# The end of a fused attention and soft-MoE kernel put in another order: last group's maxima, combine transposes, splits, and layer two

## The chip, the core and the metric

The kernel runs on one core of a Trainium2 chip. The metric is the device time of one execution in microseconds. Three runs of the kernel before the change took 1510.94, 1512.75 and 1512.81 us; the median is 1512.75 us. One further execution was recorded by the hardware profiler.

## The reference

The outputs of an attention without softmax, times its gate `u`, are the tokens of a soft mixture of experts. 8 batches of 2496 positions give N = 19968 tokens of 256 numbers; there are 8 experts with 4 slots each, so 32 slots, and hidden layers of 1024.

```python
scores = (1.0 / S) * np.matmul(z, z.transpose(0, 2, 1))
attn = np.maximum(scores, 0.0) ** 2
x = (u * np.matmul(attn, v)).reshape(N, D)

logits = x @ phi                       # N x 32
d = exp(logits - logits.max(0));  d /= d.sum(0) + 1e-09   # over tokens
slot_input = (d.T @ x).reshape(E, S_per_e, D)
for e in range(E):
    h = np.maximum(slot_input[e] @ w1[e], 0.0)
    slot_out[e] = h @ w2[e]
c = exp(logits - logits.max(1));  c /= c.sum(1) + 1e-09   # over slots
return c @ slot_out
```

The maxima and sums of `d` run over all tokens. So the experts can start only when the last token's logits are known, and every output needs the experts.

## The kernel before

**Attention.** Each batch is cut into chunks of up to 512 queries; the last batch ends in two chunks of 256. A chunk is worked off in 5 key steps `p` of two half steps `s`. In a half step PE multiplies scores (`sc`), ACT and DVE square and split them in a high and a low part (`ph`, `pl`), and PE adds their products with `v` into `acc` in PSUM. At a chunk's end `finish_chunk` multiplies `acc` with `ut` on DVE into `xg`, the tokens.

**The soft-MoE work beside it.** Tokens are gathered in groups of 1024 (`xg_[q]`, q from 0 to 18, and a last group of 512). For each full group the generator `groups(q)` makes logits, running maxima (`runmax`), exponentials, transposes of the tokens (`tr` into `xt`, line 313 on), the combine weights (kept unnormalised by slot but divided by their sum, in `cw`), and running slot sums, which `add_up` (line 385) rescales and adds into `slot_acc`. The generator stops at each `yield`; its steps are called from the list `work`, one per half step with `2 * p + s > 1`. All these use one two-bank PSUM buffer of the pool `ms_ps`, in turn.

**The order.** `InOrder` (line 47) wraps PE, ACT and DVE. Every operation called through it keeps the order in which the program names it on its engine. Almost all operations go through it, so the profile shows them at line 47 and they are told apart by their tiles. `between_last(s)` (line 510) puts work of its own between the last two half steps.

**The last group** (from line 552): logits `lg_last`, maximum, exponential `E_last`, transposes of both, slot sums `sl_last` added to the rescaled `slot_acc`, then a normalisation by the sums (`pn`) and by the maxima of the four row groups (`fac`, `fpad`, `fsel`). It ends in `sT` (a part of the tile `tiny`), the slots' inputs in the layout that layer 1 needs.

**The experts.** `layer1(eg, h)` makes 16 matmuls of 512 columns in four blocks (`h`), with a `relu` on ACT; `turn_hidden` transposes a block (`hT`) with a copy on DVE; `layer2(c, eg)` makes 64 small matmuls into `po`, for half `c` of the 256 output columns.

**Outputs.** `outputs(c, ·)` spreads `po` over the partitions (`so`) and splits it into `soh` and `sol`. `turn(k, ·)` transposes 8 of the 39 blocks of `cw` (`cT`), which `split_hi` (ACT) and `split_lo` (DVE) split into `ch` and `cl`. `tokens(c, u, ·)` is one unit: 12 matmuls into `pf`, a copy of one half by ACT and of the other by DVE into `ot`, and an output transfer by SP. `UNITS` has two units of 0.5 MiB, eight of 1 MiB, and one of 0.75 MiB; they are run for both halves `c`, 22 transfers in all. `ot` has four buffers. Before the change, turns and splits of `cw` stand between the units, and `layer2(1, ·)` between units 0 and 4:

```python
    outputs(0, ms_ps.tile([P, 512], F32, tag="ms", name="so4_0"))
    tokens(0, UNITS[0], some)
    tokens(0, UNITS[1], some)
    layer2(1, 0)
    next_turn(1)
    tokens(0, UNITS[2], some)
    layer2(1, 1)
    tokens(0, UNITS[3], some)
    next_turn(2)
```

**Weights.** 32 loads of 0.5 MiB (`w`): 16 in the last chunks into buffers of the pool `blk`, and behind them ten into the pool `wx` and six more into `blk` as attention's tiles come free; `ch` and `cl` take buffers of `blk` too.

Of the kernel before, what the change touches and what calls it, by code (L numbers as in the profile page):

```python
# [50 lines left out]
def attn_soft_moe_kernel(ctx, tc, uT, v, zz, phi, ww, outT):  # L51
# [63 lines left out]
    esel = cpool.tile([P, E_, NS], F32, name="esel")  # L115
# [9 lines left out]
    def constants():  # L125
# [3 lines left out]
        nc.gpsimd.memset(esel, 0.0)  # L129
        nc.gpsimd.memset(rsel, 0.0)  # L130
        for h in range(4):
            rows = slice(h * NS, (h + 1) * NS)
            nc.gpsimd.tensor_copy(
                esel[rows, :, 0:SE], ident[rows, rows].rearrange("k (e s) -> k e s", s=SE)
            )
            nc.gpsimd.tensor_copy(ssel[rows], ident[rows, rows])
# [126 lines left out]
    def finish_chunk(b, ch, acc):  # L263
# [3 lines left out]
        while s < n:  # L267
# [4 lines left out]
            dve.tensor_mul(xg_[q][:, :, o : o + w], acc[:, :, s : s + w], ut[:, :, s : s + w])  # L272
# [22 lines left out]
    def groups(q):  # L295
# [38 lines left out]
        yield  # L334

# [74 lines left out]
    def turn(k, ps):  # L410

        for i in range(min(8, NG - 8 * k)):
            for h, rows in enumerate(HALF):
                pe.transpose(
                    ps[:, h, i * 64 : (i + 1) * 64], cw[rows, 8 * k + i], ident[rows, rows]
                )
        return ps
# [3 lines left out]
    def split_hi(k, ps):  # L421
        hi = blk.tile([P, 8, P], F32R, tag="blk", name=f"ch_{k}")
        ng = min(8, NG - 8 * k)
        px = ps[:, :, : ng * 64].rearrange("p h (g n) -> p h g n", g=ng)
        act.copy(hi[:, :ng].rearrange("p g (h n) -> p h g n", h=2), px)
        parts[k] = hi, px

    def split_lo(k):
        hi, px = parts[k]
        lo = blk.tile([P, 8, P], F32R, tag="blk", name=f"cl_{k}")  # L430
        ng = min(8, NG - 8 * k)
        dve.tensor_sub(
            lo[:, :ng].rearrange("p g (h n) -> p h g n", h=2), px,
            f32(hi[:, :ng]).rearrange("p g (h n) -> p h g n", h=2),
        )
# [72 lines left out]
    xps, turned = [], []  # L508
# [44 lines left out]
    x = xg_.pop(q)  # L553
    lg = sc_ps.tile([P, QC], F32, tag="sc", name="lg_last")
    for c in range(2):
# [5 lines left out]
    turn_x(xps[0], x, 0, range(2, 4))  # L561

    tiny = wk.tile([P, 2, 1024], F32, tag="xg", name="tiny").rearrange("p a b -> p (a b)")
    sT = tiny[:, 0:512].rearrange("p (c k) -> p c k", c=2)
    fpad = tiny[:, 512:768]
    fsel = tiny[:, 768:800]
    fac, rs = tiny[:, 800:801], tiny[:, 802:804]
    mrow = tiny[0:1, 1024 : 1024 + 5 * NS].rearrange("p (t s) -> p t s", s=NS)
    ET = tiny[:, 1280:1408]
    nc.gpsimd.memset(sT, 0.0)  # L570
    m = wk.tile([P, 5], F32, tag="m", name="m_last")
    L = wk.tile([P, 2 * P], F32, tag="L", name="L_last", bufs=1)[:, 0:P]
    E = wk.tile([P, 2 * P], F32, tag="E", name="E_last", bufs=1)[:, 0:P]
    mnew, mold = runmax[q % 2], runmax[(q + 1) % 2]
    snew, sold = slot_acc[q % 2], slot_acc[(q + 1) % 2]
    dve.reduce_max(m[:, 0:1], lg[:, 0:P], axis=AX.X)
    dve.tensor_max(mnew, m[:, 0:1], mold)
    dve.tensor_scalar_mul(m[:, 1:2], mnew, -1.0)
    dve.tensor_sub(m[:, 2:3], mold, mnew)
    act.activation(E, lg[:, 0:P], AF.Exp, bias=m[:, 1:2], accum_out=m[:, 4:5])  # L580
    act.activation(m[:, 3:4], m[:, 2:3], AF.Exp)
    dve.tensor_copy(L, lg[:, 0:P])


    pm = ms_ps.tile([P, 2, 512], F32, tag="ms", name="pm")
    pe.transpose(pm[0:1, 0, 0:P], mnew, ident)
    dve.tensor_reduce(
        mrow[:, 4], pm[0:1, 0, 0:P].rearrange("p (t s) -> p s t", s=NS), axis=AX.X, op=ALU.max
    )
    dve.tensor_copy(mrow[:, 0:4], mrow[:, 4].unsqueeze(1).to_broadcast([1, 4, NS]))  # L590
    et = sc_ps.tile([P, QC], F32, tag="sc", name="et_last")
    pe.transpose(et[:, 0:P], E, ident)
    dve.tensor_copy(ET, et[:, 0:P])
    pe.matmul(
        pm[:, 1, 0:1], mrow[:, 0:4].rearrange("p t s -> p (t s)"), one, start=True, stop=True
    )
    dve.tensor_sub(fac, mnew, pm[:, 1, 0:1])
    act.activation(fac, fac, AF.Exp)
    act.activation(fpad, esel.rearrange("k e q -> k (e q)"), AF.Copy, scale=fac)
    dve.tensor_scalar_mul(fsel, ssel, fac)  # L600
    sl = acc_ps.tile([P, 2, QC], F32, tag="acc", name="sl_last")
    for t in range(4):
        pe.matmul(
            sl[t * NS : (t + 1) * NS, 0, 0:D], ET[:, t * NS : (t + 1) * NS], xt[:, 0, t],
            start=True, stop=True,
        )
    dve.scalar_tensor_tensor(
        snew[:, D : D + 1], sold[:, D : D + 1], m[:, 3:4], m[:, 4:5], op0=ALU.mult, op1=ALU.add
    )
    dve.scalar_tensor_tensor(  # L610
        snew[:, 0:D], sold[:, 0:D], m[:, 3:4], sl[:, 0, 0:D], op0=ALU.mult, op1=ALU.add
    )

    pn = ms_ps.tile([P, 2, 512], F32, tag="ms", name="pn")
    for eg in range(2):
        pe.matmul(
# [215 lines left out]
```

## Time and profile before

| what | us |
|---|---|
| median of three runs | 1512.75 |
| the profiled execution's own time | 1512.82 |
| its span, first to last instruction | 1510.6 |
| PE busy | 1476.4 |
| DVE busy | 1107.5 |
| ACT busy | 1022.5 |
| last `acc` ended, `xg` started | 1421.27 |
| first matmul of layer 1 | 1428.15 |
| first output transfer issued | 1448.27 |
| bytes written | 20.45 MB |

The profile of an execution is a page of totals, and views of the same trace. The chain is the row of work that ended last, followed back from the end. The timeline lists instructions with the idle time before them and what released them in brackets. The windows give busy times of the engines in a stretch, with the clock that TensorE was granted (1.00 is full). PE is TensorE's matmuls and PEld its weight loads, ACT is ScalarE, DVE VectorE, POOL GpSimd, and SP the engine that issues the transfers. All times are in us from the span's start.

### The profile page before, as it was taken

To read this page: it belongs to the slowest core of one execution; us is meant where nothing else is said; L and a number is where in the kernel's file an instruction comes from. 1 tells how busy PE (TensorE), PEld (TensorE's weight loads), DVE (VectorE), ACT (ScalarE), POOL (GpSimd) and SP (SyncE) were. 2 spreads that over 40 slices of the span, in tenths; PEclk is the share of its full clock that TensorE was granted. 3 is DMA by queue.
4 is the path that set the end of the run, shared out by engine and by line. 5 is a ranking of instruction groups with operands and counts; after the bars stand their busy time and mean duration, and the time that the engine had idled before them with its cause. 6 is when DMAs were issued, how large, how long until landed. Compare 5 with 4: busy or idle time off the path is not lost.

```text
span 1510.6 us, 36846 instructions
## 1 busy us (share of the span) xinstructions
PE 1476.4 (98%) x14749; PEld 1245.1 (82%) x14749; DVE 1107.5 (73%) x2193; ACT 1022.5 (68%) x1976; POOL 4.3 (0%) x26
## 2 busy tenths in 40 slices
PE   8999999999999999999999999999999999999984
PEld 6988888889988888889888888888988898788753
DVE  6878776878678776787778776787768787676544
ACT  7777766867677766777667766677667766665433
POOL 0000000000000000000000000000000000000000
PEclk9999999999999999999999999999999999999985
DMA  3112101121001210112101110021101140000858
GB/s 127 36 30 57 54 24 30 31 68 50 15 22 50 56 36 15 37 50 57 35 16 50 49 50 16 22 57 49 36 16 36 50 150 23 15 15 9 311 219 356
DMA packets 36651, 91.53 MB, mean 61 GB/s; under 512 B 3712, under 2 KB 6272, under 8 KB 34432
## 3 DMA queue, kind: packets, MB, share of 16 engines
q1 hardware_dynamic: 36480, 89.18, 18.6%
q8 instruction: 116, 1.90, 0.6%
q14 instruction: 55, 0.45, 0.1%
HBM read 68.71 MB, written 20.45 MB: 59 GB/s over the span
## 4 chain that ended last, share of the span: by engine, by line
PE 96%; DMA 1%; DVE 1%; ACT 1%; issue 0%; DVEq 0%; ACTq 0%; SPq 0%; POOLq 0%
PE acc L47 71%; PE sc L47 19%; PE lg L47 2%; PE tr L47 1%; DMA outT<-ot 1%; PE pf L47 1%; PE h L654 1%; PE po L676 0%; ACT ot L47 0%; PE le L47 0%; DVE ot L47 0%; DVE cl L47 0%; PE cT L47 0%; ACT ch L47 0%; DMA cw<-in_zz 0%; PE hT L666 0%
## 5 line engine op out<-in xcount | busy, mean ns | idle before, releaser
L47 PE MATMUL acc<-ph,v 64*128 64x512 f32 (+2 forms) x6396 | 1007.8, 382 | 0.1
L47 PEld LDWEIGHTS acc<-ph,v 64*128 64x128 f32 x6396 | 644.6, 184 | 94.8 <-POOLq L250 0.3
L47 ACT ACTIVATE r<-sc 128x512 f32<-128x512 f32 (+2 forms) x820 | 429.1, 575 | 364.6 <-PE sc L47 355.7
L47 PE MATMUL acc<-pl,v 64*128 64x512 f32 (+2 forms) x3198 | 654.7, 381 | 0.1
L47 DVE TENSOR_TENSOR pl<-r,ph 128x512 fp32r<-128x512 f32 (+5 forms) x820 | 546.4, 666 | 68.3 <-DVE ph L47 0.9
L47 DVE CAST ph<-r 128x512 fp32r<-128x512 f32 (+2 forms) x820 | 335.6, 409 | 259.6 <-ACT r L47 258.5
L47 ACT ACTIVATE r<-r 128x512 f32<-128x512 f32 (+2 forms) x820 | 454.9, 610 | 0.0
L47 PEld LDWEIGHTS acc<-pl,v 64*128 64x128 f32 x3198 | 336.2, 184 | 48.0 <-DVE pl L47 0.5
L47 PE MATMUL sc<-z,z 64*128 64x512 f32 (+2 forms) x1920 | 273.5, 384 | 0.0
L47 PEld LDWEIGHTS sc<-z,z 64*128 64x128 f32 x1920 | 184.2, 185 | 32.2 <-issue 6.6
L47 PE MATMUL sc<-z 64*128 64x512 f32 (+2 forms) x480 | 68.8, 385 | 0.0
L47 ACT COPY xt<-tr 128x1024 f32<-128x1024 f32 x38 | 38.6, 1015 | 28.2 <-PE tr L47 28.1
L47 DVE TENSOR_TENSOR v<-vr,v 128x512 fp32r<-128x512 f32 x80 | 54.9, 686 | 0.5
L47 DVE TENSOR_TENSOR xg<-acc,ut 128x1024 f32<-128x1024 f32 (+7 forms) x56 | 48.7, 893 | 4.2 <-PE acc L47 4.2
L47 PEld LDWEIGHTS sc<-z 64*128 64x128 f32 x480 | 45.9, 185 | 7.1 <-issue 1.6
L47 DVE TENSOR_TENSOR z<-zr,z 64x512 fp32r<-64x512 f32 x70 | 48.1, 687 | 2.0
L47 ACT CAST v<-vr 128x512 fp32r<-128x512 f32 x80 | 49.4, 617 | 0.0
L47 ACT CAST z<-zr 64x512 fp32r<-64x512 f32 x70 | 43.4, 620 | 1.7
L47 DVE COPY ot<-pf 128x1024 f32<-128x1024 f32 (+2 forms) x22 | 24.2, 1102 | 23.8 <-PE pf L47 11.9
L47 ACT COPY ot<-pf 128x1024 f32<-128x1024 f32 (+2 forms) x22 | 20.1, 916 | 30.8 <-PE pf L47 16.6
L47 PE MATMUL pf<-ch,soh 32*128 32x512 f32 (+2 forms) x88 | 20.2, 612 | 12.9 <-ACT ot L47 10.1
L47 PEld LDWEIGHTS tr<-ident,xg 64*128 64x128 f32 x608 | 25.0, 139 | 6.1 <-issue 2.3
(121 smaller groups left out, 420.1 us busy)
## 6 DMA issues: line engine op xcount, KB each, us to landing
vr<-in_v SPq DMA_DIRECT2D x80, 256.0 KB, 2.7
w<-in_w SPq DMA_DIRECT2D x32, 512.0 KB, 6.7
outT<-ot SPq DMA_DIRECT2D x16, 1024.0 KB, 5.7
ut<-in_uT SPq DMA_DIRECT2D x31, 512.0 KB, 3.7
zr<-in_zz SPq DMA_DIRECT2D x35, 256.0 KB, 2.6
ut<-in_uT SPq DMA_DIRECT2D x8, 448.0 KB, 3.5
outT<-ot SPq DMA_DIRECT2D x4, 512.0 KB, 4.2
outT<-ot SPq DMA_DIRECT2D x2, 768.0 KB, 6.4
```

The lines of the kernel that those rows point to most:

```text
L47: return lambda *a, **k: self.tc.keep_in_program_order(f(*a, **k))
L654: nc.tensor.matmul(ps[j * NS : (j + 1) * NS], sT[:, c, (4 * eg + j) * NS : (4 * eg + j + 1) * NS], w_raw[w][:, k], start=(c == 0), stop=(c ...
```

## The change

All of it acts at the end. (a) Group 18 gets one more `yield` ahead of its token transposes, and `work` seven entries for a group. (b) In the last chunk the multiplication into `xg` is done for each half of the columns apart. (c) `between_last` transposes eight blocks of `cw` in each of the last two half steps, and copies them back into `cw`. (d) The last group keeps its own maxima; old and new sums have their own factors (`fac`, `fsel`) and are added by six matmuls in PSUM; the normalisation goes into `sT`, so the `relu` has no scale. (e) The transposes of blocks 16 to 31 of `cw` stand as `fill(n)` between the steps of the last group. (f) Four of the five splits stand beside layer 1. (g) Layer 1's four blocks stand together, then the hidden transposes and `layer2(0, ·)`. (h) `layer2(1, ·)` is cut into four pieces, one behind each of units 0 to 3.

```diff
-                work.extend([lambda it=it: next(it, None)] * 6)
+                work.extend([lambda it=it: next(it, None)] * 7)
...
+        if q == NQG - 2:
+
+            yield
...
     def between_last(s):
...
-            turn_x(xps[0], xg_[NQG - 1], 0, range(2))
+        turn_x(xps[0], xg_[NQG - 1], 0, range(s, s + 1))
+        c8 = cw[:, 8 * s : 8 * s + 8]
+        if s == 0:
+            ps = acc_ps.tile([P, 2, QC], F32, tag="acc", name="cT_0")
+            turn(0, [ps[:, h] for h in range(2)])
+            act.copy(halves(c8), ps.rearrange("p h (g n) -> p h g n", g=8))
         else:
-            turned.append(turn(0, acc_ps.tile([P, 2, QC], F32, tag="acc", name="cT_0")))
+            ps = [sc_ps.tile([P, QC], F32, tag="sc", name=f"cT_1_{h}") for h in range(2)]
+            turn(1, ps)
+            for h, copy in enumerate((act.copy, dve.tensor_copy)):
+                copy(halves(c8)[:, h], ps[h].rearrange("p (g n) -> p g n", g=8))
...
+    def fill(n):
+        for i in [next(fills) for _ in range(n)]:
+            pe.transpose(
+                turned[i // 8][:, i // 4 % 2, i % 4 * P : (i % 4 + 1) * P], cw[:, 16 + i], ident
+            )
...
+    fill(4)
+    turn_c(0)
+    logits(0)
+    logits(1)
+    turn_c(1)
+    fill(2)
+    copy_c(0)
...
+    dve.tensor_reduce(mneg[:, 0:1], lg[:, 0:P], axis=AX.X, op=ALU.max, negate=True)
...
+    act.activation(E, lg[:, 0:P], AF.Exp, bias=mneg[:, 0:1])
...
-    act.activation(fpad, esel.rearrange("k e q -> k (e q)"), AF.Copy, scale=fac)
+    act.activation(fac, mneg, AF.Exp, scale=-1.0, bias=mtop)
...
+    for z, k in (sold, 1), (snew, 0):
+        pe.matmul(
+            tot, z[:, D : D + 1].to_broadcast([P, P]), fsel[:, k],
+            start=(k == 1), stop=(k == 0), skip_group_check=True,
+        )
+        for c in range(2):
+            pe.matmul(
+                sums[:, c * NS : (c + 1) * NS], z[:, c * P : (c + 1) * P], fsel[:, k],
+                start=False, stop=(k == 0), skip_group_check=True,
+            )
+    dve.tensor_scalar_add(norm, tot, 1e-9)
+    dve.reciprocal(norm, norm)
+    dve.tensor_mul(
+        sT[:, :, :, 0:SE], sums.rearrange("p (c e s) -> p c e s", c=2, s=SE),
+        norm.rearrange("p (e s) -> p e s", s=SE).unsqueeze(1).to_broadcast([P, 2, E_, SE]),
+    )
+    fill(4)
...
+    split_hi(2, whole[2])
+    for i, k in enumerate((3, 0, 1, None)):
+        if k is not None:
+            split_hi(k, whole[k])
+        split_lo((2, 3, 0, 1)[i])
+        hs[divmod(i, 2)] = layer1(*divmod(i, 2))
...
+    turn_hidden(0, 0, hs[0, 0])
+    turn_hidden(0, 1, hs[0, 1])
+    turn_hidden(1, 0, hs[1, 0], spare[:, 0])
+    next(last)
+    layer2(0, 0)
+    next(last)
+    turn_hidden(1, 1, hs[1, 1])
+    next(last)
+    layer2(0, 1)
...
+    so = slots_out(0)
...
+    turn(4, [cT[:, h] for h in range(2)])
+    spread_out(0, so, ms_ps.tile([P, 512], F32, tag="ms", name="so4_0")[:, 0:P])
...
+    for i in range(4):
+        tokens(0, UNITS[i], some)
+        layer2(1, i // 2, range(4 * (i % 2), 4 * (i % 2) + 4))
+    so = slots_out(1)
+    tokens(0, UNITS[4], some)
+    spread_out(1, so, po[:, 0, D : D + P])
+    tokens(0, UNITS[5], some)
+    split_hi(4, cT[:, :, : NG % 8 * 64].rearrange("p h (g n) -> p h g n", n=64))
+    split_lo(4)
```

On PE, behind attention's last `acc`, these are the rows of before: logits (`lg_last`), token transposes (`tr_last`), the maximum's row (`pm`), the transposed exponentials (`et_last`), the slot sums, and the first block of `h`.

```order
L47 MATMUL acc_21527<-pl_19_21846,v_9_18771 128x256
L47 MATMUL lg_last<-xg_21525,phi_sb 32x128 x8
L47 MATMUL tr_last<-ident,xg_21525 128x64 x8
L47 MATMUL pm<-ident,runmax_87 1x128
L47 MATMUL et_last<-ident,E_last 128x128
L47 MATMUL pm<-one,tiny 128x1
L47 MATMUL sl_last<-xt,tiny 32x256 x4
L47 MATMUL pn<-slot_acc_85,tiny 128x1 x2
L47 MATMUL sl_last<-tiny,slot_acc_85 128x32 x2
L654 MATMUL h_0_22093<-w_20831,tiny 32x512 x2
```

The same place on PE in the changed kernel; `cT<-ident,cw 128x128` are the fillers.

```order
L47 MATMUL cT_22030<-ident,cw 128x128 x4
L47 MATMUL tr_last_22033<-ident,xg_21519 128x128 x2
L47 MATMUL lg_last<-xg_21519,phi_sb 32x128 x8
L47 MATMUL tr_last_22033<-ident,xg_21519 128x128 x2
L47 MATMUL cT_22030<-ident,cw 128x128 x2
L47 MATMUL pm<-ident,tiny 1x128
L47 MATMUL cT_22030<-ident,cw 128x128 x2
L47 MATMUL et_last<-ident,E_last 128x128
L47 MATMUL cT_22064<-ident,cw 128x128 x2
L47 MATMUL pm<-one,tiny 128x1
L47 MATMUL et_last<-xt,tiny 32x256 x4
L47 MATMUL cT_22064<-ident,cw 128x128 x2
```

Sixteen transposes have moved from between the output units to here (the last four stand behind the six sums that follow), and the two `pn` are gone.

On PE behind layer 1, in the changed kernel, the four transposes of each hidden block are followed by `lt` (the transposed logits `L_last`, into the tile `spare`) and by layer 2:

```order
L47 MATMUL h_1_22145<-w_21867,tiny 32x512 x2
L47 MATMUL hT_0_22169<-ident,hidden 128x128 x4
L47 MATMUL hT_1_22175<-ident,hidden 128x128 x4
L47 MATMUL spare<-ident,hidden 128x128 x4
L47 MATMUL spare<-ident,L_last 128x128
L47 MATMUL po<-w_21993,hT 32x128 x2
```

Before, `lt` stood behind the first block of `h`, and each `hT` between blocks of `h` or of `po`; now three `hT` stand together, and `lt` writes the tile that the third has just written.

On ACT, from the last group to the first output copy, before (`hs` are the hidden blocks, `cw` the last combine weights):

```order
L47 ACTIVATE tiny<-esel,tiny 128x256
L47 CAST ch_22065<-cT_21933 128x2x8x64
L659 ACTIVATE hs_0_22102<-h_0_22093,tiny 128x512
L659 ACTIVATE hs_1_22118<-h_1_22109,tiny 128x512
L47 ACTIVATE cw<-cw 128x128
L659 ACTIVATE hs_0_22136<-h_0_22127,tiny 128x512
L659 ACTIVATE hs_1_22157<-h_1_22148,tiny 128x512
L47 COPY so_22241<-po_22091 128x256
```

And in the changed kernel:

```order
L47 CAST ch_22099<-cT_22030 128x1024
L47 CAST ch_22101<-cT_22064 128x1024
L47 ACTIVATE hidden<-h_0_22105 128x512
L47 CAST ch_22115<-cw 128x1024
L47 ACTIVATE hidden<-h_1_22119 128x512
L47 CAST ch_22129<-cw 128x1024
L47 ACTIVATE hidden<-h_0_22133 128x512
L47 ACTIVATE hidden<-h_1_22145 128x512
L47 ACTIVATE cw<-cw 128x128
L47 COPY so_22273<-po 128x256
```

Four splits (`ch`) stand now in front of and between the hidden blocks; before there was one here, and three more between the output units.

More of the change, by code (lines that the diff above doesn't have):

```diff
@@ L413, in turn, with halves, split_hi @@
             for h, rows in enumerate(HALF):
[L414 to L417, printed above, removed]
+                pe.transpose(ps[h][:, i * 64 : (i + 1) * 64], cw[rows, 8 * k + i], ident[rows, rows])
     parts = {}
-    def split_hi(k, ps):
+    def halves(t, g=8):
+        return t[:, :g].rearrange("p g (h n) -> p h g n", h=2)
+    def split_hi(k, px):
         hi = blk.tile([P, 8, P], F32R, tag="blk", name=f"ch_{k}")
-        ng = min(8, NG - 8 * k)
-        px = ps[:, :, : ng * 64].rearrange("p h (g n) -> p h g n", g=ng)
-        act.copy(hi[:, :ng].rearrange("p g (h n) -> p h g n", h=2), px)
+        act.copy(hi if k < 4 else halves(hi, NG % 8), px)
         parts[k] = hi, px
@@ L560, in attn_soft_moe_kernel @@
             )
[L561 to L571, printed above, removed]
@@ L594, in attn_soft_moe_kernel @@
+    fill(2)
+    ps = acc_ps.tile([P, 2, QC], F32, tag="acc", name="et_last")
+    turned.append(ms_ps.tile([P, 2, 512], F32, tag="ms", name="cT_3"))
+    pe.transpose(ps[:, 0, 0:P], E, ident)
+    act.copy(ET, ps[:, 0, 0:P])
+    fill(2)
     pe.matmul(
-        pm[:, 1, 0:1], mrow[:, 0:4].rearrange("p t s -> p (t s)"), one, start=True, stop=True
+        pm[:, P : P + 1], mrow.rearrange("p t s -> p (t s)"), one, start=True, stop=True
     )
-    dve.tensor_sub(fac, mnew, pm[:, 1, 0:1])
-    act.activation(fac, fac, AF.Exp)
@@ L620, in attn_soft_moe_kernel @@
-    for c in range(2):
-        pe.matmul(
-            sl[:, 1, c * NS : (c + 1) * NS], snew[:, c * P : (c + 1) * P], fsel,
-            start=True, stop=True,
-        )
-    dve.tensor_copy(
-        sT.rearrange("p c (e k) -> p c e k", k=NS)[:, :, :, 0:SE],
-        sl[:, 1, 0 : 2 * NS].rearrange("p (c e s) -> p c e s", c=2, s=SE),
-    )
-    dve.tensor_scalar_add(rs, pn[:, 0, 0:2], 1e-9)
-    dve.reciprocal(rs, rs)
-    split_hi(0, turned[0])
-    split_lo(0)
-    att_ps.close()
-    moe.close()
+    act.copy(snew[:, 0:D], ps[:, 1, 0:D])
```

173 lines of the change are left out of this document (79 added, 94 removed).

## The prediction

> **What bounds the kernel now.** I read the page first: the span, the busy time of each engine, and the chain that ended last.
>
> ```profile
> span 1510.6 us, 36846 instructions
> PE 1476.4 (98%) x14749; PEld 1245.1 (82%) x14749; DVE 1107.5 (73%) x2193; ACT 1022.5 (68%) x1976; POOL 4.3 (0%) x26
> PE 96%; DMA 1%; DVE 1%; ACT 1%; issue 0%; DVEq 0%; ACTq 0%; SPq 0%; POOLq 0%
> ```
>
> PE is the bound of the attention, which fills all but the last 90 us. The change edits the end, where 98% is no guide. So I read the chain from there on, in order of time (start, length, what).
>
> ```profile
> 1419.51 0.50 PE cT L47 x16
> ...
> 1421.27 0.70 DVE xg L47
> ...
> 1422.01 0.63 PE lg_last L47 x12
> ...
> 1425.80 0.52 ACT tiny L47
> ...
> 1426.36 0.61 PE pn L47 x4
> 1426.97 0.54 PE sl_last L47 x4
> ...
> 1428.15 3.79 PE h L654 x16
> 1431.94 0.41 PE lt_last L47
> ...
> 1435.65 1.85 PE h L654 x16
> 1437.51 0.59 PE hT L666 x4
> ...
> 1440.54 1.88 PE po L676 x64
> ...
> 1443.01 1.93 PE po L676 x64
> 1444.96 0.38 ACT so L47
> ...
> 1445.38 0.71 PE so L47 x4
> ...
> 1446.89 0.61 PE pf L47 x12
> ...
> 1447.55 0.59 ACT ot L47
> ...
> 1450.51 1.02 ACT ch L47
> 1451.56 1.23 DVE cl L47
> 1452.78 1.14 DVE ot L47
> ...
> 1462.39 1.86 PE pf L47 x12
> ...
> 1483.66 7.61 DMA outT<-ot
> ```
>
> Four stretches: attention ends with `xg` at 1421.27; a chain of small steps for the last group of tokens runs 6.88 us to the first `h` at 1428.15; the expert layers run to 1444.94; then come the outputs. Up to the piece at 1483.66 the outputs' chain goes through PE, ACT and DVE, and from there through the output transfers. The same in the windows view, with the timeline's row of the first output transfer (windows: start:end, length, busy time of PE, PEld, DVE, ACT, POOL, granted clock, DMA share, GB/s).
>
> ```profile
> 1448.27 8.33 SPq L756 DMA_DIRECT2D outT<-ot  x4
> 1448.30:1478.00 29.70, 22.77 (x270) 14.64 (x270) 15.49 (x15) 13.63 (x16) 0.00 (x0) 0.66 0.70 284
> 1478.00:1507.70 29.70, 14.83 (x132) 9.53 (x130) 12.88 (x12) 10.21 (x12) 0.00 (x0) 0.61 0.99 405
> 1507.70:1510.60 2.90, 0.00 (x0) 0.00 (x0) 0.00 (x0) 0.00 (x0) 0.00 (x0) 0.50 0.05 21
> ```
>
> The page's DMA section has the bytes:
>
> ```profile
> HBM read 68.71 MB, written 20.45 MB: 59 GB/s over the span
> ```
>
> From 1478 the DMA engines are full at 405 GB/s. In the 29.7 us ahead of that they are 70% used, so about 9 us of transfer time is lost. That is the largest sum on the table: whatever is taken from the work ahead of 1478 is gained, until the transfers are full from the first one on.
>
> **The change part by part.** The sums are against the profiled execution, 1512.82 us for a span of 1510.6, so 2.2 lie around the span; the median shown is 1512.75, 0.07 less.
>
> *Attention's end.* The timeline has one stall of PE in the last chunks:
>
> ```profile
> 1388.86 0.71 PE L47 MATMUL tr<-ident,xg 64*128 64x64 f32 x16 [1.64 <-DVE slot_acc L47]
> 1391.20 0.65 PE L47 MATMUL tr<-ident,xg 64*128 64x64 f32 x15
> ```
>
> The transposes of group 18 stood 1.64 us for a buffer that `slot_acc`'s additions on DVE still read. One more `yield` puts them a half step later, which is 2.3 us by the two rows (the second set belongs to the next half step): longer than the stall. I take −1.64. Bounds: 0 if DVE is as late a half step on; nothing in the rows lets more than the stall be gained. Against it, 32 instead of 16 `cT` transposes stand between the last half steps: +0.50 by the row at 1419.51. The new ACT and DVE copies back into `cw` lie behind attention's last scores, where both engines idle. Attention thus ends at 1421.27 − 1.64 + 0.50 = 1420.13.
>
> *Last group's chain.* Gone from the path: the widening of the factor (1425.80, 0.52) and `pn` (1426.36, 0.61), 1.13 together. Added: four more of the small sums, 4 × 0.54/4 = 0.54, and 16 filling transposes. A transpose of this size costs 0.59/4 = 0.147 by the `hT` row, so 2.35 for all. Four lie under the wait for `xg`, most others under waits for DVE and ACT (one path step is waited for at nearly each of them), but PE works in order, so one that starts just ahead of the awaited data delays it. I take 0.56 for that, so the chain stays at 6.85, near its 6.88. Bounds: −0.6 (fillers all hidden) to +1.8 (all of them on the path). Layer 1 then starts at 1427.0 instead of 1428.15.
>
> *Layer 1.* The granted clock decides:
>
> ```profile
> 1423.80:1427.20 3.40, 2.27 (x20) 1.43 (x19) 1.80 (x8) 1.92 (x6) 0.00 (x0) 1.00 1.03 410
> 1427.20:1430.60 3.40, 2.75 (x15) 1.27 (x18) 0.74 (x4) 0.01 (x1) 0.00 (x0) 0.51 1.03 411
> 1430.60:1434.10 3.50, 3.50 (x21) 0.69 (x17) 1.53 (x3) 0.69 (x1) 0.00 (x0) 0.50 1.02 408
> ```
>
> It was 0.5 from 1427.2 to 1434.1, so the first block of `h` took 3.79 and a later one 1.85. The window ahead of the fall had PE busy 2.27 of 3.40 us. The fillers add up to 2 us of PE work to that stretch, and attention ends 1.1 earlier in it. I take the clock as held: 4 × 1.85 = 7.4, so layer 1 ends at 1434.4. The four pairs of splits beside it (`ch` 1.02 on ACT, `cl` 1.23 on DVE, rows at 1450.51 and 1451.56) come to 4.1 and 4.9 us, with four `relu` of 0.69 on ACT, inside 7.4.
>
> ```profile
> L659 ACT ACTIVATE hs<-h,tiny 128x512 f32<-128x512 f32 x4 | 2.8, 688 | 10.6 <-PE h L654 10.6
> ```
>
> They need buffers of weights that layer 1's first block reads, so they start some 0.5 us in. If that cover went, `hT`'s copies on DVE would be late by the excess; ACT's sum of 6.9 leaves 0.5.
>
> The Trainium skill, page "TensorE: Matmul & The Clock Gate", speaks on this in two sections. "Part 1: The HAM clock gate" puts the fall after an idle window of about 3.4 us and the rise after a busy one; the 3.4 us steps agree with the trace, but here a window that was two thirds busy was enough for the fall. "Part 4: PE-mode transpose" says that a transpose doesn't count as busy in the same way, which speaks against fillers made of transposes. By that rule the clock falls as before, the case of the first rival below; no run so far shows which holds.
>
> *Between layer 1 and the outputs.* Three blocks of `hT` together, 3 × 0.59 = 1.77, to 1436.2. Then a new wait: the order shows `lt`'s transpose, which goes into the bank that the third `hT` copy still reads, ahead of layer 2 on PE.
>
> ```profile
> L667 DVE COPY hT<-hT 128x512 f32<-128x512 f32 x4 | 2.8, 692 | 7.0 <-PE hT L666 7.0
> ```
>
> Three copies of 0.69 from 1435.07 end at 1437.15, so PE stands 0.9, and all of layer 2 behind it. Then `lt` 0.2, layer 2's first half 1.88, `hT` 0.59, the other half 1.93: 1441.8. `cT_4`'s transposes 0.6 (beside `so`'s copy), `so` 0.71, the two splits of 0.3 each, the first `pf` 0.61, `ot` 0.69 and 0.1 of issue give a first output transfer at 1445.2, against 1448.27.
>
> *Outputs.* Before, units waited for turns and splits (1450.51, 1451.56, then `ot` 1452.78 behind them: 2.3 us of DVE and ACT for each of four blocks). These now lie beside layer 1 but for `cT_4`'s. A unit of 1 MiB is `pf` (half of 1.86 as the clock is full, 0.93 to 1.0), the longer copy 1.23 and 0.1: 2.35. One piece of layer 2 behind each of units 0 to 3 (half of 1.93, 0.97) fits under that copy. A MiB takes 1.05/0.405 = 2.59 in transfer, so from the third unit on the transfers are the slower ones. Unit 6 waits for `cT_4`'s `cl` to free its bank; that is about 1 us, which the first transfers' queue nearly hides. The first transfer of before, in the DMA view from 1447 to 1450:
>
> ```profile
> outT<-ot SPq DMA_DIRECT2D x1, 512.0 KB, 2.6
> ```
>
> Of its 2.6 us, 1.3 are transfer (0.52/0.405), so bytes flow 1.3 after the issue. From the issue at 1445.2 I count two 0.5 MiB units and four of 1 MiB done by 1461.0, and the other 15.2 MB at 405 to 409 GB/s done by 1498.4, plus the 2.75 us that follow the last full window. The span ends at 1501.0, with ±0.5 for the bubble. Total 1501.0 + 2.2 = **1503.2**: −9.6, of which 3.0 by the earlier first output and 6.6 by fuller transfers.
>
> **Rivals.** *The clock falls all the same.* For: the fillers are transposes, and in the window of the fall PE had been busy for 67%. Against: PE now has more work in this stretch and `h` starts at 1427.0, so a whole window of 1427.2 to 1430.6 is busy and should lift it one window sooner than before, where it was 2.75 of 3.40. Half clock for 3.4 us does half of its work, +1.8: **1505.0**; two windows give 1506.7.
>
> *The stall does not go.* The extra pop moves all later steps of group 18 too, and what DVE owes can meet them elsewhere; or the queue pops shift and nothing moves. Then −1.64 is lost: **1504.8**.
>
> *The transfers aren't filled.* Should the clock be at half from the first units, a unit is 1.86 + 1.9 = 3.8 of PE, and units 2 to 5 arrive 1.2 us too late each: +5, **1508**. If the first ten units kept the former 284 GB/s, only the earlier start were left: 1512.8 − 3.0 = 1509.8. For: the clock was 0.66 over that stretch before. Against it:
>
> ```profile
> 1451.10:1454.60 3.50, 3.21 (x84) 2.36 (x76) 2.35 (x2) 1.34 (x2) 0.00 (x0) 1.00 0.40 154
> 1454.60:1458.00 3.40, 2.37 (x34) 1.25 (x28) 2.50 (x3) 2.83 (x3) 0.00 (x0) 1.00 0.98 402
> 1458.00:1461.40 3.40, 2.81 (x16) 1.77 (x16) 1.45 (x3) 0.73 (x4) 0.00 (x0) 0.50 0.99 407
> ```
>
> With PE busy 3.21 of 3.50 the clock stayed, and it fell behind a window of 2.37; the new units 0 to 3, with 1.0 of `pf` and 0.97 of layer 2 in 2.35, hold as much as the first.
>
> *Slower.* The clock falls at 1427 and stays down through the layers: layer 1 +7.8 (4 × 3.79), layer 2 +3.8, transposes, `so` and `pf` some +3, then the slow units' +5: 1503.2 + 19.6 = **1522.8**. It ends slower than before once half clock has lasted some 21 us without a break (9.6 of 14.6 us lost over the 32 us that this stretch would then take). For: 0.66 on the outputs' first half. Against: 1430.6 to 1434.1 above, one whole busy window and the clock was back.
>
> **How the numbers follow.** Forecast 0.45; clock falls for one or two windows 0.27; stall stays 0.11; transfers not filled 0.13, a third of it above 1509.7; slower 0.04. The predicted time is the forecast's, 1503.2, with a range of its own of 1502.1 to 1505.0 (chain −0.6 to +1.8, bubble −0.5). The wide range goes from 1500.8 (chain −0.6, bubble −0.5, the wait of 0.9 ahead of `lt` gone, and 0.4 for 15.2 MB at the 411 GB/s of 1427.20) to 1508.0, where the case of half clock in the units begins to be left out. About 0.2% (3 us) is what a measurement of this kernel can tell from no change: faster 0.91, the same 0.05, slower 0.04.
>
> **What would show it.** Right: no wait over 0.5 us ahead of group 18's `tr`; the last `acc` near 1420.1; first `h` near 1427.0, all four blocks at 1.85; a wait of about 0.9 ahead of `lt`; first output near 1445.2; DMA share above 0.9 from about 1450. Wrong: a first block of `h` near 3.8 (the clock), a first `h` later than 1428 (fillers on the path), a chain through `pf` and `ot` instead of the transfers up to 1475 (units not filled), or landings further apart than 2.6 us for a MiB.

## The result and the profile after

| | before | after |
|---|---|---|
| median, us (6 runs each) | 1511.13 (1509.12 to 1512.81) | 1503.61 (1502.30 to 1504.72) |
| profiled execution, us | 1512.82 | 1502.30 |
| span, us | 1510.6 | 1500.0 |

The ratio of the times is 0.9949, with a 95% interval of 0.9936 to 0.9962: the changed kernel is faster by 7.5 us between the medians. The forecast was 1503.2. Between the two profiled executions it is 10.5 us, as that of before lies at the top of its kernel's runs and that of after at the bottom.

The page of the changed kernel, the same lines as were read of before:

```profile
span 1500.0 us, 36817 instructions
PE 1469.9 (98%) x14733; PEld 1247.2 (83%) x14733; DVE 1106.9 (74%) x2192; ACT 1023.7 (68%) x1979; POOL 3.5 (0%) x21
DMA 2%; PE 0%; DVE 0%; ACT 0%; issue 0%; DVEq 0%; SPq 0%; ACTq 0%
```

The chain that ended last no longer leads through PE into attention. It begins in the outputs, with one wait for `cl` and the matmuls of unit 6, and from 1462.52 on it is transfers for the most part (three pieces of 7.79, 7.68 and 9.23 us, and the last one). The timeline of the changed kernel shows the steps that the prediction named (start, length, engine, operation, and in brackets the idle time before it and what ended it):

```profile
1388.82 0.69 PE L47 MATMUL tr<-ident,xg 64*128 64x64 f32 x15
...
1419.30 0.76 DVE L47 TENSOR_TENSOR xg<-acc,ut 128x256 f32<-128x256 f32 x2 [0.54 <-PE acc L47]
...
1426.84 1.49 PE L47 MATMUL h<-w,tiny 128*32 128x512 f32 x12 [0.60 <-DVE tiny L47]
...
1433.84 1.09 PE L47 MATMUL hT<-ident,hidden 128*128 128x128 f32 x8
...
1436.47 0.33 PE L47 MATMUL spare<-ident,L_last 128*128 128x128 f32 x1 [1.10 <-DVE hT L47]
...
1444.57 19.90 SPq L798 DMA_DIRECT2D outT<-ot  x10
...
1457.06 0.54 PE L47 MATMUL pf<-ch,soh 32*128 32x512 f32 x2 [2.84 <-DVE cl L47]
```

The wait of 1.64 ahead of `tr` is gone. Attention ends (`xg`) at 1419.30 instead of 1421.27; layer 1 starts at 1426.84 instead of 1428.15 and lasts 7.1 us instead of 11.8 (with hidden transposes between its blocks); the first output transfer is issued at 1444.57 instead of 1448.27. Two waits are new, 1.10 ahead of the last logits' transpose and 2.84 at unit 6.

The windows view tells what the transfers did behind the first issue. The last three columns are the granted clock, the DMA share and GB/s. First the changed kernel:

```profile
1444.60:1450.60 6.00, 5.85 (x142) 4.14 (x134) 2.90 (x3) 2.61 (x3) 0.00 (x0) 1.00 0.65 264
1450.60:1459.00 8.40, 5.26 (x50) 3.47 (x52) 4.48 (x6) 4.24 (x6) 0.00 (x0) 0.90 1.02 421
1459.00:1462.00 3.00, 3.00 (x30) 1.70 (x26) 2.71 (x3) 2.10 (x4) 0.00 (x0) 0.70 0.64 262
1462.00:1497.00 35.00, 18.54 (x146) 11.69 (x144) 14.69 (x14) 11.86 (x14) 0.00 (x0) 0.58 1.01 415
```

And the kernel before, from its first issue to where its transfers became full:

```profile
1448.30:1454.30 6.00, 5.71 (x124) 4.03 (x128) 3.05 (x3) 2.51 (x3) 0.00 (x0) 1.00 0.45 178
1454.30:1465.50 11.20, 8.39 (x82) 5.27 (x74) 6.30 (x6) 5.67 (x8) 0.00 (x0) 0.66 0.88 362
1465.50:1478.00 12.50, 8.67 (x68) 5.33 (x68) 6.14 (x7) 5.45 (x6) 0.00 (x0) 0.50 0.65 264
```

A share below 1 is transfer time lost. Before, that is 3.3 us in the first 6, 1.3 in the next stretch and 4.4 in the third: 9.0. After it is 2.1 in the first 6 us and 1.1 in the hole behind unit 5: 3.2.

### The profile page after: what moved, and what is told of

Its sections match the earlier page's. It is cut to its first block, busy times and chain, and to the rows that moved or that the text cites. A ratio compares the mean times of both kernels' runs of the same rounds, so it can differ in the third digit from the quotient of the medians.

```text
span 1500.0 us, 36817 instructions
## 1 busy us (share of the span) xinstructions
PE 1469.9 (98%) x14733; PEld 1247.2 (83%) x14733; DVE 1106.9 (74%) x2192; ACT 1023.7 (68%) x1979; POOL 3.5 (0%) x21
```

## The experiments

Twelve runs on the chip. For each run the table gives the median and the number of its timed executions, and from the timeline of its one profiled execution: the end of attention's last `acc`, the length of layer 1 (first to last `h`), the issue of the first output transfer, and the time from there to the span's end. In before and `before_yield` layer 1 includes the hidden transposes between its blocks. The last column shows by itself what the output stage takes, since nothing that comes ahead of it moves it much: the seven profiles with the changed kernel's outputs as they are lie between 55.3 and 55.7.

| run | median us | last acc | layer 1 | first issue | issue to end |
|---|---|---|---|---|---|
| before | 1511.13 (6) | 1421.2 | 11.8 | 1448.27 | 62.3 |
| after | 1503.61 (6) | 1419.3 | 7.1 | 1444.57 | 55.4 |
| control | 1502.47 (5) | 1419.1 | 7.1 | 1444.46 | 55.5 |
| control2 | 1503.18 (5) | 1418.4 | 8.1 | 1444.79 | 55.6 |
| no_yield | 1504.48 (5) | 1421.0 | 7.1 | 1446.30 | 55.6 |
| before_yield | 1508.19 (11) | 1418.8 | 10.3 | 1445.24 | 60.2 |
| no_fill | 1506.02 (7) | 1419.1 | 9.3 | 1448.43 | 55.3 |
| unit6 | 1501.70 (5) | 1418.6 | 7.1 | 1443.94 | 54.4 |
| lt_later | 1501.26 (5) | 1419.7 | 8.8 | 1445.43 | 55.3 |
| both | 1499.90 (5) | 1418.5 | 8.2 | 1443.69 | 54.2 |
| split1_late | 1502.91 (5) | 1418.9 | 7.1 | 1444.18 | 56.5 |
| layer2_whole | 1505.12 (5) | 1419.6 | 8.8 | 1446.58 | 56.1 |
| turn3_late | 1506.54 (11) | 1418.6 | 9.9 | 1446.94 | 57.5 |
| esel_back | 1504.69 (1) | 1419.5 | 8.7 | 1446.44 | 55.7 |

**The control, twice.** The changed kernel as it is.

> The changed kernel once more, as the measure for the runs beside it and to see its two groups of times (so far 1502.3 to 1502.8 and 1504.5 to 1504.7 us). Theory: the upper group is the granted clock falling to half for one window of 3.4 us somewhere ahead of the first output, worth some 2 us; a profile of that group then has a half-clock window ahead of 1444.6. Rival: the groups differ in the output transfers; then the clock's falls are the same as in the first profile (first fall at 1457.4) and the landings lie further apart. Median 1502 to 1505.

> The changed kernel again, as the measure beside the next runs: 1502.3 to 1504.7 us, most often 1502.3 to 1502.8.

With the six executions of the first measurement there are sixteen: nine from 1501.80 to 1502.76, one at 1503.18, and six from 1504.45 to 1504.72. Neither control's profile is of the upper group. That of `control2` (1502.64 us) has a window of half clock all the same, from 1424.7 to 1428.1, so such a window alone does not make an execution one of the upper group: here attention had ended 0.7 earlier than in `control`, and the window cost 1.0. The mean granted clock, on record for every execution, is 0.988 in all of the lower group but that one (0.986), and 0.986 or 0.987 in the upper group. The runs `lt_later` and `esel_back` below show a window of half clock at the place where it costs more.

**The stall of group 18, from both sides.** Taken out of the changed kernel (`no_yield`), and put alone into the kernel before (`before_yield`).

```diff
-                work.extend([lambda it=it: next(it, None)] * 7)
+                work.extend([lambda it=it: next(it, None)] * 6)
...
-        if q == NQG - 2:
-
-            yield
```

> The changed kernel without the extra yield, and six entries in the list of work as before; the result is the same. Theory (the stall ahead of group 18's transposes was all real path): PE waits 1.6 us at group 18's transposes again, all later work moves by it, and the time is 1.6 to 2.1 us above the control, the small waits at the chunk's end included. Rival (the stall was hidden, or another wait takes its place): within 0.5 us of the control.

> The kernel before with the extra yield alone (and seven entries in the list of work); the result is the same. Theory (the stall is real path in either kernel): no wait ahead of group 18's transposes, the last acc 1.6 to 2.0 us earlier, and the time lower than before by as much. Rival (behind it the last group, the weights' loads or the clock take it back): the last acc is earlier, but the first h or the first output transfer is not, and the time is within 0.5 us of before.

The row of `tr` in `no_yield`'s timeline, and the first of it in `before_yield`'s:

```profile
1388.24 0.72 PE L47 MATMUL tr<-ident,xg 64*128 64x64 f32 x16 [1.63 <-DVE slot_acc L47]
```

```profile
1388.68 0.21 PE L47 MATMUL tr<-ident,xg 64*128 64x64 f32 x1
```

The wait came back with its 1.63, and went in the other kernel. `no_yield` is 2.0 us above the control beside it by the medians, and 1.9 by the two profiled spans, both at full clock up to the outputs. `before_yield` against before has the ratio 0.9985 (0.9976 to 0.9994), 2.8 us between the medians. That is more than the 1.6 to 2.0 expected. In its profile the last `acc` came 2.4 earlier than in before's, of which 0.4 to 0.5 was there at the start already, and the output stage was shorter by 2.1, with less time at half clock; so the yield is worth some 2.0 there too. The theory held: the stall was path in either kernel. The price is somewhat more than the wait itself, as the theory's upper end had it: aligned by the order of the `pl` steps, the changed kernel gained 1.57 us at the stall, 0.24 at the small waits of the next chunk boundary, and 0.24 soon after 1413. `no_yield`, aligned in the same way, gained none of the three, so they come with the yield.

**The fillers.**

```diff
+    act.copy(turned[0].rearrange("p h (g n) -> p (h g) n", n=P), cw[:, 16:24])
     fills = iter(range(16))
...
     def fill(n):
         for i in [next(fills) for _ in range(n)]:
-            pe.transpose(
-                turned[i // 8][:, i // 4 % 2, i % 4 * P : (i % 4 + 1) * P], cw[:, 16 + i], ident
-            )
+            pass
...
     split_hi(2, whole[2])
+    act.copy(whole[3], cw[:, 24:32])
```

> The 16 filling transposes are left out; two copies by ACT of untransposed blocks stand in their place, so combine groups 16 to 31 are not computed as the reference has them. Theory 1 (fillers lie partly on the path, and the clock does not need them): the first matmul of h comes 0.4 to 0.8 us earlier after the last acc (7.58 us in the first profile), layer 1's blocks stay at 1.7 to 1.9 us, and the time falls by as much. Theory 2 (fillers hold the clock): the clock is at half from about 1427, the first block of h takes up to 3.8 us, and the time is 1 to 3.5 us above the control.

The windows of `no_fill` from the last `acc` on:

```profile
1419.30:1422.70 3.40, 2.01 (x23) 1.09 (x23) 1.80 (x8) 1.25 (x5) 0.00 (x0) 1.00 1.02 410
1422.70:1426.10 3.40, 2.91 (x17) 2.02 (x18) 0.58 (x3) 2.23 (x4) 0.00 (x0) 0.51 1.04 416
1426.10:1429.50 3.40, 2.28 (x14) 1.55 (x18) 0.77 (x3) 0.28 (x1) 0.00 (x0) 0.50 1.02 402
1429.60:1433.00 3.40, 3.40 (x20) 0.90 (x16) 1.98 (x2) 1.83 (x3) 0.00 (x0) 0.50 1.03 411
```

Theory 2 held: the clock was at half for three windows, from 1422.7 to 1433.0, the last group's chain (9.4 from the last `acc` to the first `h`, instead of 7.6) and layer 1 (9.3 instead of 7.1) both took longer, and the time is 3.6 us above the control's. The two copies by ACT are not what made the chain longer: they began at 1418.36 and 1425.34, while PE did work that waits for neither, and the six sums behind 1424.5, on PE alone, took 2.8 us instead of 1.5. Nor does the place of the clock's windows explain the fall. The clock rose at 16.46 us at the start here, between the 16.32 of `no_yield` and the 16.79 of `control`, which both kept it; `turn3_late` below, with eight fillers, rose at 15.61 and lost it for two windows, where `unit6` rose at 15.65 and kept it. The mean granted clock agrees for the executions without a profile: 0.984 to 0.986 in the seven of `no_fill`, 0.986 to 0.988 in the sixteen of the changed kernel. So the 16 fillers do more than free places between the output units: they keep the clock up, or let it fall for a shorter time.

**Unit 6.**

```diff
     tokens(0, UNITS[5], some)
+    tokens(0, UNITS[6], some)
     split_hi(4, cT[:, :, : NG % 8 * 64].rearrange("p h (g n) -> p h g n", n=64))
...
-    units = [(0, u) for u in UNITS[6:]] + [(1, u) for u in UNITS[2:] + UNITS[1::-1]]
+    units = [(0, u) for u in UNITS[7:]] + [(1, u) for u in UNITS[2:] + UNITS[1::-1]]
...
-        tokens(c, u, [more_ps, more_ps] if i % 2 else [rest_ps, rest_ps])
+        tokens(c, u, [rest_ps, rest_ps] if i % 2 else [more_ps, more_ps])
```

> Unit 6 is put ahead of the split of the last combine block and into the buffers of units 0 to 5, so it waits for neither; the result is the same. Theory (the wait of 2.84 us of PE at unit 6 makes a hole in the transfers, whose landings went from 2.54 to 4.04 us apart there): the hole goes, transfers are full from unit 2 on, 1.2 to 1.6 us below the control. Rival (the hole only moves to unit 7, or the ramp is given back at the four buffers of ot): within 0.4 us of the control.

Its windows at the same distance from the first issue as those of after:

```profile
1443.90:1449.90 6.00, 5.86 (x146) 4.07 (x134) 2.83 (x3) 2.61 (x3) 0.00 (x0) 1.00 0.65 261
1449.90:1458.30 8.40, 6.25 (x58) 3.72 (x54) 4.91 (x6) 4.38 (x6) 0.00 (x0) 0.87 1.00 414
1458.30:1461.30 3.00, 3.00 (x32) 2.10 (x24) 2.48 (x3) 2.02 (x2) 0.00 (x0) 0.50 1.01 418
```

The hole of 0.64 is now 1.01, and the output stage takes 54.4 us instead of 55.4 or 55.5. The hole's price is 1.0 us; the medians give 0.8, below the 1.2 to 1.6 expected, with executions of both kernels overlapping.

**The wait ahead of `lt`.**

```diff
-    next(last)
     layer2(0, 0)
     next(last)
+    next(last)
```

> The changed kernel with the transpose of the last logits moved behind the first half of layer 2, so PE no longer waits for the third copy of a hidden block ahead of it; the result is the same. Theory (the wait of 1.10 us is path): layer 2 starts when the second copy is done, 0.6 us earlier, the first output transfer comes at 1443.9 instead of 1444.5, and the time falls by about 0.6 us, to 1501.9 where the control's median was 1502.47. Rival (the copies on DVE or the last combine block become late instead): the first transfer stays at 1444.5 and the time within 0.2 us.

The windows of its profiled execution, and two rows of its timeline:

```profile
1424.30:1427.70 3.40, 2.67 (x22) 1.92 (x25) 0.93 (x4) 1.23 (x2) 0.00 (x0) 0.99 1.04 413
1427.70:1431.10 3.40, 3.40 (x20) 0.87 (x16) 1.63 (x2) 1.49 (x2) 0.00 (x0) 0.50 1.02 404
1431.10:1434.50 3.40, 3.40 (x36) 1.04 (x32) 2.28 (x3) 2.70 (x5) 0.00 (x0) 1.00 1.02 407
```

```profile
1436.90 0.60 PE L47 MATMUL spare<-ident,hidden 128*128 128x128 f32 x4
1437.43 1.96 PE L47 MATMUL po<-w,hT 128*32 128x128 f32 x64
```

Layer 2 follows the third `hT` without a wait. Layer 1 was longer by 1.7 in this one execution, for the clock fell to half for one window in it; this execution took 1503.15 us, and the four others 1500.36 to 1501.63. That fits the upper group of times: one window of half clock within layer 1. With these 1.7 us taken off, the time from the last `acc` to the first issue is 24.05 us where the control has 25.31, a gain of 1.26 instead of the 0.6 expected. The profile of `both` below gives the same: 25.14, less the 1.1 by which its layer 1 is longer, is 24.0. The median is 1.2 below the first control's, though the two were not run side by side.

**Both edits.** The edits of `unit6` and `lt_later` together.

> The edits of unit6 and of lt_later together; the result is the same. Theory (both are on the path that fills the transfers, one after the other): their gains add, 1.4 to 2.2 us below the control's 1502.47. Rival (the transfers' ramp is bound by something later): no better than unit6 alone, 1501.7.

Median 1499.90, 2.6 below the first control; the ratio to before is 0.9931 (0.9919 to 0.9944), against 0.9952 (0.9938 to 0.9965) for the control. The gains add, to the upper end and a little over. The output stage is the shortest of all, 54.2. All five of its executions (1499.58 to 1499.96, and one of 1501.21) lie below the fastest of the changed kernel's sixteen, 1501.80.

**One split back between the units.**

```diff
-    for i, k in enumerate((3, 0, 1, None)):
+    for i, k in enumerate((3, 0, None, None)):
...
-        split_lo((2, 3, 0, 1)[i])
+        if i < 3:
+            split_lo((2, 3, 0)[i])
...
     for i in range(4):
+        if i == 2:
+            split_hi(1, whole[1])
+            split_lo(1)
         tokens(0, UNITS[i], some)
```

> The changed kernel with one of the four splits, that of combine groups 8 to 15, moved from beside layer 1 to between units 1 and 2, as a split stood before; the result is the same. Theory (the splits between the units were what kept the transfers from being full): the third transfer's issue moves from 1448.5 to about 1450.7, as the split's ACT and DVE steps take 1.02 and 1.23 us ahead of its copies, and the time rises by 1.5 to 2.3 us. Rival (the units' slack against the transfers, 0.2 to 0.3 us each, hides it, and the gain comes from the pieces of layer 2): within 0.5 us of the control.

Neither quite. The first windows:

```profile
1444.20:1450.20 6.00, 5.35 (x120) 3.51 (x116) 3.23 (x4) 2.94 (x4) 0.00 (x0) 1.00 0.52 209
1450.20:1458.60 8.40, 5.25 (x74) 3.40 (x66) 4.79 (x5) 3.99 (x6) 0.00 (x0) 0.88 1.00 414
```

The share of the first 6 us falls from 0.65 to 0.52, 0.8 us of transfer, and the output stage takes 56.5, 1.0 to 1.1 more. The third transfer was issued 4.85 us behind the first instead of 4.05. The median rose by 0.4 against the first control, where the executions scatter by 2. The theory's mechanism shows; its price was overrated by half, because the timeline has ACT's part at 1445.52, beside the unit's matmuls, and DVE's at 1446.60, beside a piece of layer 2.

**Layer 2's second half in two pieces.**

```diff
-        layer2(1, i // 2, range(4 * (i % 2), 4 * (i % 2) + 4))
+        if i % 2:
+            layer2(1, i // 2)
```

> The changed kernel with layer 2's second half in two whole pieces of 64, behind units 1 and 3, in place of four; the result is the same. Theory (a piece of 1.0 us fits under a unit's copies, one of 1.95 doesn't): the third and fifth transfers are issued some 0.5 to 0.9 us later, the time 0.3 to 1.0 us above the control. Rival (the ramp hides it): within 0.3 us of the control.

The first window of the output stage, where the changed kernel has a share of 0.65:

```profile
1446.60:1452.60 6.00, 4.83 (x115) 3.62 (x119) 2.17 (x3) 2.06 (x3) 0.00 (x0) 1.00 0.55 216
```

The output stage takes 56.1, 0.5 to 0.7 more than after and the controls. The third transfer was issued 4.77 us behind the first instead of 4.05, 0.7 later and within the theory's range; the fifth 9.93 instead of 8.67, 1.3 later and above it. The median is 1.9 above the control beside it, but the five executions lie 4 us apart (1503.44 to 1507.62), and layer 1 took 8.8 in the profiled one, for the clock; so I take the trace's 0.5 to 0.7.

**Two turns and splits back between units 6 to 9.** As before: `cT`, `ch` and `cl` of the blocks 24 to 31 behind unit 6, and of 32 to 38 behind unit 8.

```diff
-    fills = iter(range(16))
+    fills = iter(range(8))
...
-    for i, k in enumerate((3, 0, 1, None)):
+    for i, k in enumerate((0, 1, None, None)):
...
-    tokens(0, UNITS[5], some)
-    split_hi(4, cT[:, :, : NG % 8 * 64].rearrange("p h (g n) -> p h g n", n=64))
-    split_lo(4)
+    for k in (3, 4):
+        tokens(0, UNITS[2 * k - 1], some)
+        tokens(0, UNITS[2 * k], some)
+        cT = tn_ps.tile([P, 2, 512], F32, tag="tn_ps", name=f"cT_{k}")
+        turn(k, [cT[:, h] for h in range(2)])
...
+        act.copy(halves(hi, g), px)
+        dve.tensor_sub(halves(lo, g), px, halves(f32(hi), g))
...
-    units = [(0, u) for u in UNITS[6:]] + [(1, u) for u in UNITS[2:] + UNITS[1::-1]]
+    units = [(0, u) for u in UNITS[9:]] + [(1, u) for u in UNITS[2:] + UNITS[1::-1]]
```

> The changed kernel with the combine blocks 24 to 38 turned and split between the units 6 and 7 and 8 and 9, as before, and so only 8 fillers beside the last group; the result is the same. In the changed kernel the issues of units 6 to 10 come within 5.5 us, before within 13.2. Theory (turns and splits between the units, one after the other through PE, ACT and DVE, kept the transfers empty there): these issues take 9 us or more again, the DMA share has holes up to unit 10, and the time is 3 to 5 us above the control. Rival (the half clock of 1458 to 1481.9 did it, and the queue of transfers now hides a split): within 1 us of the control. The eight missing fillers may let the clock fall ahead of layer 1, which shows in the first h and is to be taken off.

```profile
1452.90:1464.00 11.10, 6.77 (x74) 3.76 (x70) 6.63 (x7) 5.50 (x7) 0.00 (x0) 0.95 1.00 413
1464.00:1473.00 9.00, 7.67 (x64) 5.39 (x68) 4.41 (x4) 3.73 (x4) 0.00 (x0) 0.50 0.69 282
```

The issues of units 6 to 10 took 12.4 us, and the transfers lost 2.8 us from 1464 to 1473, where the changed kernel loses 1.1 at unit 6. The output stage takes 57.5, 2.1 us more. The other part of the 3.4 us over the control beside it comes from the clock: with eight fillers layer 1 took 9.9. So the theory's holes are there, but they are smaller than those of before (4.4 us), and they come later, as the units ahead kept the transfers full (share 1.00 up to 1464, where before had 0.88 up to 1465.5).

**A set-up on POOL.** In the first profile everything was 0.27 us earlier from 21 us on.

```diff
+    esel = cpool.tile([P, E_, NS], F32, name="esel")
...
+        nc.gpsimd.memset(esel, 0.0)
         nc.gpsimd.memset(rsel, 0.0)
...
+            nc.gpsimd.tensor_copy(
+                esel[rows, :, 0:SE], ident[rows, rows].rearrange("k (e s) -> k e s", s=SE)
+            )
```

> The changed kernel with the set-up of the tile esel on POOL put back, which nothing reads any more; the result is the same. The changed kernel runs 0.27 us ahead of before from the ninth split of attention's start on, 21 us into the span. Theory (POOL's ten operations for esel delayed the constants and through them a transfer or a wait there): that split comes at 21.38 again, 0.27 later. Rival (something else of the start moved): it stays at 21.10.

It came at 21.35, as the theory had it, and yet the theory falls: the same row of kernels without this set-up lies anywhere from 20.25 (`control2`) to 21.58 (`lt_later`). What moves it is in the timelines' first rows, matmuls of one form, first in `control2`, then in `lt_later`:

```profile
14.60 0.57 PE L47 MATMUL acc<-pl,v 64*128 64x512 f32 x1
15.04 0.40 PE L47 MATMUL acc<-pl,v 64*128 64x512 f32 x1
```

```profile
17.10 0.62 PE L47 MATMUL acc<-pl,v 64*128 64x512 f32 x1
17.59 0.56 PE L47 MATMUL acc<-pl,v 64*128 64x512 f32 x1
18.19 0.39 PE L47 MATMUL acc<-pl,v 64*128 64x512 f32 x1
```

They go from 0.62 to 0.39 us at a time that differs from one execution to the next, 15.0 in the one and 17.9 in the other: the clock's rise at the start. The 0.27 us are no part of the change. The time of this run is that of the upper group, 1504.69 us: the clock's rise came late at the start, and it fell for one window from 1427.0, so layer 1 took 8.75. The two together, 0.4 and 1.7 against the control, are the 2.1 us between the groups.

## Why the forecast was right, step by step

| step | forecast | measured in the profile of after |
|---|---|---|
| wait at group 18 | −1.64 | −1.57, and −0.48 of small waits |
| attention's end | 1420.1 | 1419.3 |
| last group's chain | 6.85 | 7.54 |
| first `h` | 1427.0 | 1426.84 |
| layer 1 | 7.4 | 7.1 |
| wait ahead of `lt` | 0.9 | 1.10 |
| first output transfer | 1445.2 | 1444.57 |
| transfers full from | unit 2 | unit 2, but for a hole at unit 6 |
| span's end | 1501.0 | 1500.0 |

The mechanism of each term held in this profile, but the close agreement of the sums is in part luck: attention ended 0.8 earlier than forecast, the chain took 0.7 more, layer 1 took 0.3 less and the wait ahead of `lt` 0.2 more. In the outputs the loss at unit 6, about 1.0, was made up for in part by a rate of 415 GB/s in the full windows, where 405 to 409 had been taken; 55.8 us were forecast and 55.4 measured. The sizes that were off:

*The last group's chain* is 0.7 longer than I had it. The term "four more of the small sums, 4 × 0.54/4 = 0.54" is mis-sized: the row had four records, but the order shows two matmuls there, so one costs 0.27. The six sums of the changed kernel took 1.52 us, 0.98 more than the two of before where 0.54 had been added, which is 0.44 of the 0.7; the rest was not traced:

```profile
1424.24 0.85 PE L47 MATMUL et_last<-tiny,slot_acc 128*128 128x32 f32 x6
1424.93 0.83 PE L47 MATMUL et_last<-tiny 128*128 128x32 f32 x6
```

*The bubble at unit 6* was forecast as a wait of about 1 us that the queue nearly hides. PE waited 2.84, and the transfers lost about 1.0 (`unit6`). *The bound of attention's gain* was wrong: I wrote that nothing in the rows lets more than the stall be gained, and 2.05 was gained against a stall of 1.64, some 0.24 of it at the chunk boundary, whose small waits I had not counted. *The wait ahead of `lt`* came as forecast, 1.10 for the third copy of a hidden block, but not for the place that was given: the kernel has that block in `spare[:, 0]` and `lt` in `spare[:, 1]`, the other half of the tile. *The span's end* was added up loosely: 1498.4 and 2.75 are 1501.15, and the row of the last window has 2.90.

*The clock* was the term with the most weight, and it was right for about half of the executions. Of the ten profiles of kernels with all 16 fillers, that of after included, five kept the full clock from the last `acc` to the first output, and five fell to half for one window; `turn3_late`, with eight fillers, fell for two. The first rival was given 0.27 against 0.45, and is about as frequent as the forecast. Its price, +1.8, was right where the window lay within layer 1: 1.7 in `lt_later`. In `control2` it began ahead of it and cost 1.0. So the median of 1503.61 is near the forecast's 1503.2 by luck: of the six executions three took 1502.30 to 1502.76 and three 1504.45 to 1504.72, and the median is the middle between the two groups, where none of the six lies. For the held clock the forecast was 0.4 to 0.9 too high. The forecast fall, 9.6, counts from a profiled execution at the top of before's times; between the medians it is 7.5.

On this the Trainium skill's page "TensorE: Matmul & The Clock Gate" had two rules. "Part 4: PE-mode transpose" would have transposes not count as busy in the same way; `no_fill`, with 2.01 of 3.40 us busy ahead of its fall and three windows at half, shows that these transposes do help to hold the clock. "Part 1: The HAM clock gate" says that the window runs freely and that its position varies from run to run; the rise at the start between 15.0 and 17.9 agrees. The rule there, that the clock falls after at least one idle window, is too narrow for this case: it fell behind windows with PE busy 2.67 (`lt_later`) and 3.10 (`control2`) of 3.40.

*The rivals that fell*: the stall did go (`before_yield`, `no_yield`). The transfers did fill. The slower case would have needed some 21 us at half clock; without any filler it was 10.2.

*What the gain consists of.* Between the two profiled spans there are 10.6 us: 0.3 from the position of the clock's rise at the start, 1.7 net by attention's end (2.0 of waits less the added transposes), 1.7 between there and the first output, and 6.9 in the output stage. The 1.7 ahead of the first output come from the clock: before stood at half from 1427.2 to 1434.1, and its first two blocks of `h` took 3.79 and 2.79 where the other two took 1.92 each, 2.7 us together. By this estimate the new order by itself makes that stretch about 1.0 longer at the same clock. Of the 6.9 in the output stage, the three edits that were undone one at a time account for 1.0 (one of the four early splits), 0.6 (layer 2 in pieces) and 2.1 (the last two turns and splits, less the price of unit 6's wait, and with fewer fillers). These are 3.7 of the 6.9, if they add. What the splits of blocks 16 to 23 bring was not tried. The clock has a part in it that was not separated: in `before_yield` it stood at half for a shorter time in the outputs, and that stage took 60.2 instead of 62.3, in the same order.

## What to carry to other kernels

Where a kernel ends in full transfers, look for the time at which they first become full, and count a share below one as lost time: an edit ahead of that point pays by what it closes. That one behind it pays nothing is to be expected, but was not tried here. Before pricing an instruction from a row, check how many records the row counts for each instruction. Where a chain of small steps hands over to dense matmuls, work that keeps TensorE busy in the chain can be worth more than its own place, but judge it over several executions, as here the clock fell for a window in about half of them.

## What the runs showed of the hardware

Whether the clock fell ahead of the first output went with the position of its windows at the start. In the ten profiles with all 16 fillers the clock's rise at the start, by the traces' record of the granted clock, came between 15.65 and 16.95 us in the five that kept the full clock, and between 17.3 and 17.95, or at 15.0 and 15.3, in the five that lost it for a window; as the windows are 3.41 us apart (the falls ahead of the first output lasted 3.41, 6.83 or 10.24 us), 15.0 and 15.3 are the positions 18.4 and 18.7. That the position is the cause is not shown, as no run could set it. The busy time of PE in the window ahead does not decide alone, as two windows views show, the first of `control2`, where the clock fell behind the window, the second of after, where it held:

```profile
1421.30:1424.70 3.40, 3.10 (x27) 2.17 (x27) 1.07 (x6) 1.85 (x5) 0.00 (x0) 1.00 1.02 405
1424.70:1428.10 3.40, 3.24 (x18) 1.40 (x21) 0.77 (x3) 0.06 (x1) 0.00 (x0) 0.50 1.03 407
```

```profile
1423.30:1426.70 3.40, 2.81 (x26) 1.96 (x18) 1.18 (x6) 1.58 (x3) 0.00 (x0) 1.00 1.03 411
1426.70:1430.10 3.40, 3.26 (x32) 1.07 (x36) 2.12 (x3) 2.16 (x3) 0.00 (x0) 1.00 1.03 405
```

PE was busy for 3.10 of 3.40 us ahead of the fall, and for 2.81 where the clock held. What is judged in a window stays open.
